# Half tiles of v copied by GpSimd, sinks' values spread in DRAM, and values' products and scores in one piece on TensorE

## The chip, the core and the metric

The kernel runs on one core of a Trainium2 chip. Its time is the device time of one launch in microseconds (us), the median of several runs. One further execution was recorded by the hardware profiler; every row below is from that one. Engines are called PE (TensorE), DVE (VectorE), ACT (ScalarE), POOL (GpSimd) and SP (SyncE, which here only issues DMAs).

## The reference

Sliding-window attention with sinks, then a feed-forward layer with a special activation:

```python
# q, k, v: (4 batches, 8 heads, 768 positions, 64); n_sink = 4, window = 128
keep   = is_sink | in_window                      # key among the first 4, or 0 <= row - key < 128
a      = softmax(where(keep, q @ k.T / 8, -1e9))
x      = (a @ v) as (3072 tokens, 512)
h      = x @ w_in                                 # 512 -> 2048
g      = h * erf(softplus(h))
out    = g @ w_out                                # 2048 -> 512
```

All is float32. Products are kept exact enough by splitting an operand into a high and a low part and adding three products.

## The kernel before

**Tiling.** Tokens go in 12 groups of 256 (three to a batch). A group's attention is 4 steps, one for each pair of heads, 48 steps in all (s = 0 to 47). A group's feed-forward layer takes 16 slices f of the hidden dimension; two slices make one tile `h` of 128x512, so a step of attention stands beside two such tiles on PE.

**A step of attention.** `score(s)` multiplies q by k into the tile `ps` (eight products on 64x64 parts of the PE array). DVE and ACT apply the mask, take the exponential and normalise. From s = 15 on (`TT`) DVE transposes blocks into the tile `turn` (line 445, and 446 for the sinks' probabilities), which goes to DRAM and comes back in another order: one DMA `pd<-turn` (line 448) and four DMAs `pa<-pd` (line 474). POOL then makes from `pa` the tile `pz` and clears the parts of `pa` that lie outside the window (lines 490 and 499; the last two instructions of a step, the "selects", write `pa`). `av(s)` multiplies these probabilities by values on 128x64 parts of the array: 4 or 6 products of `pa` with the tile `v`, then 8 of `pz` with `vz`. `vz` is one tile for all heads in which half tiles of v stand beside the sinks' values. `core(s)` issues `av(s-2)` and then `score(s)`.

**How vz is filled.** The function `dup` (lines 298 and 300) copies two halves of each step's `v` into `vz` by two DMAs on SP's queue. At the first group of a batch, line 247 loads the first 16 rows of v for two heads into eight places of `vz` by eight DMAs of 4 KB.

**The feed-forward layer.** `hidden` fills `h` by products on the whole 128x128 array (line 739), ACT and DVE compute the activation in six passes (lines 752 to 761), DVE and POOL split it into `g` (lines 768, 769), and `project` adds it into the output tile `o` (lines 784 to 786).

**Order.** A planner gives every call a due time in units of slices (`plan`, `pos(s)`) and a priority from the table `O`. A scheduler that simulates the engines then picks, on each engine, the ready instruction with the smallest due time. On the chip each engine runs its list strictly in that order, and SP issues its DMAs strictly in its own order too: a DMA that must wait holds up all that stand behind it.

Of the kernel before, what the change touches and what calls it, by code (L numbers as in the profile page):

```python
# [9 lines left out]
F32 = mybir.dt.float32  # L10
# [9 lines left out]
P = 128  # L20
SW = 16
# [23 lines left out]

TT = 15

LATE = 31

FH = 8  # L50

PW, EA = 256, 12
O = dict(prep=-100, norm=-100, core=-300, av=-300, load=-400, dup=-100, kcopy=-50, ptrans=-200, pread=-200, phalf=-150, xfin=-100,
         hid=0, proj=900, res=500, act=-400, wl=100, wc=0, ws=300)
E = dict(ptrans=-250)
UB = 4
# [4 lines left out]
def kernel(  # L61
# [74 lines left out]
    def fast_path():  # L136
        with ExitStack() as st:
# [53 lines left out]
            nc.vector.memset(vz[P // 2 :, 0], 0.0)  # L191
            nc.vector.memset(vz[: P // 2, 1], 0.0)

            pst = pers.tile([P, RING, 2, 2, KB], F32, name="pst")

            xp, early = {}, {}
# [8 lines left out]
            def load(s, what="qk"):  # L205
                g, c = divmod(s, NPAIR)
                b, gb = divmod(g, GPB)
                d = stp.setdefault(s, {})
                if "q" in what:
                    t = raw.tile([P, 2, GT], F32, tag="kq", bufs=1, name=f"kq_{s}")  # L210
                    if s >= DT:
                        d["kq"] = t
                    else:
                        d["k"], d["q"] = (t[:, j].rearrange("p (n h d) -> p n h d", n=2, h=2) for j in range(2))
                    last = start = mark.get(("d", s - 2))
                    for j, src in enumerate((k, q)):
                        if j and start is not None:
                            last = pread(s - 2, last)
                        for h in range(2):
                            if s < DT:  # L220
                                nc.sync.dma_start(
                                    d["kq"[j]][:, :, h, :],
                                    src[b, 2 * c + h, gb * GT : (gb + 1) * GT, :].rearrange("(n p) d -> p n d", p=P),
                                )
                                continue
                            for e in range(2):
                                p0 = 64 * h + 32 * e
                                x = nc.sync.dma_start(
                                    t[p0 : p0 + 32, j, :].rearrange("p (n c) -> p n c", c=32),
                                    src[b, 2 * c + h, gb * GT : (gb + 1) * GT, 32 * e : 32 * e + 32].rearrange("(n r) c -> r n c", r=32),  # L230
                                )
                                last = mark["l", s] = follow(last, x)
                if "v" in what:
                    t = d["v"] = raw.tile([P, 3, 2, D], F32, tag="v", bufs=1 + AL, name=f"v_{s}")
                    m0 = 0 if gb == 0 else 1
                    for h in range(2):
                        x = nc.sync.dma_start(
                            t[:, 1 - m0 :, h, :],
                            v[b, 2 * c + h, gb * GT - m0 * P : (gb + 1) * GT, :].rearrange("(n p) d -> p n d", p=P),
                        )  # L240
                        follow(mark.get(("l", s)), x)
                if gb == 0 and "v" in what:
                    for z in range(2):
                        for i in range(2):
                            for h in range(2):
                                r0, e = HP * (1 - z) + 2 * SW * i + SW * h, 2 * c + h
                                nc.sync.dma_start(vz[r0 : r0 + SW, z, i, e], v[b, e, :SW, :])

            def load_v(s):
                load(s, "v")  # L250
# [43 lines left out]
            def dup(s):  # L294

                g, c = divmod(s, NPAIR)
                t, cs = stp[s]["v"], slice(2 * c, 2 * c + 2)
                nc.sync.dma_start(vz[lo, 0, :, cs], t[lo, 1:])
                x = t[hi, 1:2].broadcast_to([HP, 2, 2, D]) if g % GPB == 0 else t[hi, :2]
                nc.sync.dma_start(vz[hi, 1, :, cs], x)  # L300

            def kcopy(s):

# [42 lines left out]
            def score(s, prev):  # L346
# [22 lines left out]
                for i in range(2):  # L369
                    qt = kq[:, c, 3 + i, :]  # L370
                    kt = kq[:, c].rearrange("p n t -> p (n t)")
                    runs = ((lo, KB * i, KB + 64, X[i]), (hi, KB * i + 64, KB + 80, X[i] - 80))
                    if gb + i == 0:
                        runs = ((lo, KB, KB, X[i]), (hi, KB, KB, X[i]))
                    for hf, r0, n, x in runs:
                        for h in (1, 0):
                            r = slice(64 * h, 64 * h + 64)
                            prev = follow(
                                prev,
                                nc.tensor.matmul(ps[h][hf, x : x + n], qt[r, hf], kt[r, r0 : r0 + n], start=True, stop=True),  # L380
                            )

                i0 = int(gb == 0)
                for hf, x, y in ((lo, X[0], X[0] + KB), (hi, X[0] + 64, X[0] - 80)):
# [123 lines left out]
            def av(s):  # L508

                g, c = divmod(s, NPAIR)  # L510
                d = stp[s]
                gb = g % GPB
                if s < 2:
                    a = ps_h.tile([P, 2, GT], F32, tag="h", name=f"av_{s}")[:, 0, :]
                elif s < NE:
                    a = ps_o.tile([P, DM], F32, tag="o", name=f"av_{s}")[:, :GT]
                else:
                    a = ps_t.tile([P, GT], F32, tag="t", name=f"av_{s}")
                d["av"] = a
                vt, pz = d["v"], d["pz"]  # L520
                pa = d["pa"].rearrange("p h i t -> p h (i t)")
                ops = []
                for j, (t0, t1) in enumerate(((0, HP), (HP, 3 * HP), (3 * HP, GT))):
                    if j > 0 or gb > 0:
                        x = vt[j] if isinstance(vt, list) else vt[:, j]
                        ops.append((x, pa[:, :, t0:t1], t0))
                for i in range(2):
                    for z, hf in enumerate((lo, hi)):
                        ops.append((vz[:, z, i, 2 * c : 2 * c + 2], pz[:, :, i, hf], P * i + HP * z))
                prev = mark.get(("p", s + 1)) if 0 < s < NE - 1 else None  # L530
                for m, (x, y, t0) in enumerate(ops):
                    for h in range(2):
                        o = a[64 * h : 64 * h + 64, t0 : t0 + y.shape[-1]]
                        prev = follow(
                            prev,
                            nc.tensor.matmul(
                                o, x[:, h, :], y[:, h, :], start=(m == 0), stop=(m == len(ops) - 1), skip_group_check=True
                            ),
                        )
                return prev  # L540

            def xfin(s):
# [24 lines left out]
            for s in range(NSTEP + AL):  # L567
                if s < NSTEP:
                    for what, fn, a in (
                        ("prep", prep, max(4, s - 1) if NE <= s < 2 * NPAIR else pos(s) - 3 + (s > TT)), ("norm", norm, pos(s) + 1 + (s == 1)), ("ptrans", ptrans, pos(s) + 2),  # L570
                        ("load", load, pos(s) - 4),
                    ):
                        if what == "load":
                            if s < 2 * NPAIR:
                                continue
                            plan.setdefault(a, []).append(("load", load_v, s))
                            a -= 1
                        plan.setdefault(max(a, 0 if what == "prep" else -1), []).append((what, fn, s))
                    if s >= TT:
                        if s + 2 >= NSTEP:  # L580
                            plan.setdefault(pos(s) + 3, []).append(("pread", lambda s: pread(s, mark["d", s]), s))
                        plan.setdefault(pos(s) + 5, []).append(("phalf", phalf, s))
                    if s >= 2 * NPAIR:
                        plan.setdefault(pos(s) - 2, []).append(("dup", dup, s))
                    if s // NPAIR % GPB < GPB - 1:
                        plan.setdefault(pos(s) + (2 if s < NE else 1), []).append(("kcopy", kcopy, s))
                plan.setdefault(pos(s), []).append(("core", core, s))
# [88 lines left out]
                    fn(*args)  # L676
            for z in range(2):
                plan.setdefault(0, []).append(("kcopy", lambda s: early_dup(s), z))
            plan.setdefault(2 * NE, []).append(("dup", lambda s: next_dup(), NE))
            plan.setdefault(2, []).append(("prep", lambda s: set_rest(), NSTEP))  # L680
            for m in range(-LEAD, NG * NF + LAG + 2):
# [257 lines left out]
```

## Time and profile before

| | |
|---|---|
| time, median of 3 runs | 742.46 us (742.04 to 745.74) |
| the profiled execution's own time | 743.12 us |
| its span, first to last instruction | 741.4 us |
| mean granted clock of PE | 0.986 |
| busy: PE, DVE, ACT, POOL | 95%, 74%, 67%, 34% |

How to read the rows: a row of a timeline has the start in us, the time that a merged run of equal instructions covers, engine, line, operation, tiles written and read (`out<-in`), shape and count; in brackets the idle time of the engine before it and what ended it. SPq is SP issuing a DMA. PE records one float32 product of `av` or `ps` as two instructions, so 14 products of values are 28 rows' worth. PE's instructions are pipelined: a full-array product of `o` starts 0.23 us after the one before, one of `h` 0.12 us, although each is shown as longer. PEclk 1.00 is TensorE's full clock of 2.4 GHz, 0.50 is 1.2 GHz.

### The profile page before, as it was taken

The numbers are of one execution on the slowest core, as the hardware profiler recorded it, in microseconds if no ns is written. First come the engines' busy times: TensorE is split into PE (matmuls) and PEld (weight loads), VectorE is DVE, ScalarE is ACT, GpSimd is POOL, SyncE is SP. The second block draws the span as 40 slices with busy tenths as digits, with TensorE's granted clock in tenths as the row PEclk, the third lists the DMA queues.
The fourth block names the chain that finished last, engine by engine and source line by source line (L and its number), as shares of the span: only waits on it lengthen the run. The fifth ranks groups of instructions, "written<-read, shape, count | busy, mean of one in ns | idle before, by whom it ended". The sixth has DMA issues, their size and how long they took to land. (4 is left out here: it accounts for less than half of the span.)

```text
span 741.4 us, 16223 instructions
## 1 busy us (share of the span) xinstructions
PE 703.4 (95%) x5515; PEld 573.5 (77%) x5515; DVE 545.9 (74%) x1473; ACT 494.4 (67%) x1157; POOL 253.5 (34%) x421
## 2 busy tenths in 40 slices
PE   6789998999999899899899999999999999999996
PEld 3566656787888788788688788878888878888885
DVE  6999995787777778677678768678778678664352
ACT  4686848978875576466476667577577577576572
POOL 3421302033334334343434434334524423432221
PEclk9999999999999999999999999999999999999999
DMA  7999011112244645545453553544554553420000
GB/s 177 278 352 359 18 30 54 24 31 44 65 77 102 133 103 104 113 88 92 84 130 64 104 129 70 100 110 83 102 113 85 101 125 72 85 65 1 28 1 34
DMA packets 256379, 72.87 MB, mean 98 GB/s; under 512 B 217568, under 2 KB 248928, under 8 KB 256288
## 3 DMA queue, kind: packets, MB, share of 16 engines
q1 hardware_dynamic: 255728, 71.68, 42.1%
q8 instruction: 46, 0.75, 0.4%
q14 instruction: 45, 0.37, 0.2%
q10 hardware_dynamic: 560, 0.07, 0.1%
HBM read 48.83 MB, written 17.10 MB: 89 GB/s over the span
## 5 line engine op out<-in xcount | busy, mean ns | idle before, releaser
L739 PE MATMUL h<-xh,wt 128*128 128x256 f32 x1408 | 278.6, 286 | 3.1 <-DVE u L761 2.8
L739 PEld LDWEIGHTS h<-xh,wt 128*128 128x128 f32 x1408 | 224.9, 189 | 20.8 <-issue 11.1
L739 PE MATMUL h<-xl,wt 128*128 128x256 f32 x704 | 197.8, 281 | 0.0
L757 ACT ACTIVATE u<-r 128x512 f32<-128x512 f32 x288 | 164.1, 623 | 43.0 <-DMA out_dram<-ot 25.3
L769 POOL TENSOR_TENSOR g<-u,g 128x512 fp32r<-128x512 f32 x84 | 113.2, 1347 | 217.9 <-DVE g L768 211.3
L761 DVE SCALAR_TENSOR_TENSOR u<-u,u 128x512 f32<-128x512 f32 x168 | 132.3, 788 | 26.1 <-ACT u L757 15.9
L739 PEld LDWEIGHTS h<-xl,wt 128*128 128x128 f32 x704 | 132.9, 189 | 4.6 <-issue 1.4
L784 PE MATMUL o<-wt,g 128*128 128x512 f32 x336 | 135.5, 403 | 0.7 <-DVE g L768 0.7
L785 PE MATMUL o<-wt,g 128*128 128x512 f32 x336 | 133.9, 399 | 0.0
L786 PE MATMUL o<-wt,g 128*128 128x512 f32 x336 | 132.7, 402 | 0.4 <-POOLq L907 0.2
L402 ACT ACTIVATE pst<-pst,neg 128x144 f32<-128x144 f32 x192 | 77.5, 406 | 63.9 <-DVE neg L398 63.7
L761 DVE SCALAR_TENSOR_TENSOR u<-u,h 128x512 f32<-128x512 f32 x84 | 56.7, 676 | 52.9 <-ACT u L757 52.3
L752 ACT ACTIVATE r<-h 128x512 f32<-128x512 f32 x96 | 57.0, 594 | 47.3 <-PE h L739 41.0
L786 PEld LDWEIGHTS o<-wt,g 128*128 128x128 f32 x336 | 62.8, 190 | 16.3 <-issue 1.0
L499 POOL TENSOR_SCALAR_AFFINE_SELECT pz<-pa 64x256 f32<-64x256 f32 (+1 forms) x96 | 45.4, 473 | 86.7 <-ACT pa L460 85.7
L784 PEld LDWEIGHTS o<-wt,g 128*128 128x128 f32 x336 | 63.9, 190 | 14.1 <-ACT pst L402 0.9
L785 PEld LDWEIGHTS o<-wt,g 128*128 128x128 f32 x336 | 63.8, 190 | 11.6 <-issue 0.3
L754 ACT ACTIVATE r<-r 128x512 f32<-128x512 f32 x96 | 60.4, 629 | 2.4
L753 ACT ACTIVATE r<-r 128x512 f32<-128x512 f32 x96 | 60.5, 630 | 2.2
L490 POOL COPY pz<-pa 64x256 f32<-64x256 f32 x66 | 29.2, 442 | 75.2 <-DMA pa<-pd 74.4
L417 DVE TENSOR_SCALAR pst<-pst,sum 128x128 f32<-128x128 f32 x168 | 49.9, 355 | 1.5
L380 PE MATMUL ps<-kq 64*64 64x208 f32 (+2 forms) x768 | 48.6, 360 | 1.2 <-DVE neg L398 0.7
(97 smaller groups left out, 872.6 us busy)
## 6 DMA issues: line engine op xcount, KB each, us to landing
pd<-turn SPq DMA_DIRECT2D x33, 320.0 KB, 2.7
pa<-pd SPq DMA_DIRECT2D x132, 80.0 KB, 2.6
ws<-in_moe_w_in_dram SPq DMA_DIRECT2D x16, 512.0 KB, 7.2
ws<-in_moe_w_out_dram SPq DMA_DIRECT2D x16, 512.0 KB, 8.7
out_dram<-ot SPq DMA_DIRECT2D x24, 256.0 KB, 2.4
v<-in_v_dram SPq DMA_DIRECT2D x56, 96.0 KB, 2.3
vz<-v SPq DMA_DIRECT2D x80, 64.0 KB, 2.1
kq<-in_k_dram SPq DMA_DIRECT2D x144, 32.0 KB, 2.2
```

Of the source, the lines that this page charges most:

```text
L402: mark["e", s] = nc.scalar.activation(y, y, AF.Exp, bias=d["neg"][:, i, h : h + 1], scale=-1.0, accum_out=d["sum"][:, i, h : h + 1])
L417: nc.vector.tensor_scalar_mul(p, p, sm[:, i, h : h + 1])
L739: last = nc.tensor.matmul(o, wt[NC * j + c][:, p, fs], xt[e][:, c, :], start=(m == 0), stop=(m == len(ops) - 1))
L752: nc.scalar.activation(r, h, AF.Tanh, bias=b_t, scale=0.5)
L753: nc.scalar.activation(r, r, AF.Square, bias=b_v, scale=-0.5)
L754: nc.scalar.activation(r, r, AF.Square, bias=b_r)
L757: sq = nc.scalar.activation(u, r, AF.Square, bias=b_a[i], scale=CS)
L761: pr = nc.vector.scalar_tensor_tensor(out=acc, in0=u, scalar=CC[i] * CS**2, in1=x, op0=ALU.add, op1=ALU.mult)
L769: nc.gpsimd.tensor_tensor(gl, acc, gh.bitcast(F32), op=ALU.subtract)
L784: behind(nc.tensor.matmul(o, gh[:, ws], wt[16 + f][:, 0, :], start=(f == 0), stop=False))
L785: nc.tensor.matmul(o, gh[:, ws], wt[16 + f][:, 1, :], start=False, stop=False)
L786: nc.tensor.matmul(o, gl[:, ws], wt[16 + f][:, 0, :], start=False, stop=(f == NF - 1))
```

## The change

Three edits, and a table entry with them. `set_sinks` writes `sinks` from 32 partitions of zeros (1 MB), and then the first 16 rows of v:

```diff
+NSINK = 22
...
-O = dict(prep=-100, norm=-100, core=-300, av=-300, load=-400, dup=-100, kcopy=-50, ptrans=-200, pread=-200, phalf=-150, xfin=-100,
+O = dict(prep=-100, norm=-100, core=-300, av=-300, load=-400, dup=-100, kcopy=-50, ptrans=-200, rest=-4000, pread=-200, phalf=-150, xfin=-100,
...
+            sinks = dram.tile([B * NPAIR, P // 2, 2, 2, D], F32, tag="sinks", bufs=1, name="sinks")
...
                 if gb == 0 and "v" in what:
-                    for z in range(2):
-                        for i in range(2):
-                            for h in range(2):
-                                r0, e = HP * (1 - z) + 2 * SW * i + SW * h, 2 * c + h
-                                nc.sync.dma_start(vz[r0 : r0 + SW, z, i, e], v[b, e, :SW, :])
+                    for z, hf in enumerate((hi, lo)):
+                        nc.sync.dma_start(
+                            vz[hf, z, :, 2 * c : 2 * c + 2].rearrange("p i h d -> p i (h d)"),
+                            sinks[b * NPAIR + c].rearrange("p i h d -> p i (h d)"),
+                        )
+
+            def set_sinks():
+
+                x = vz[HP : HP + 2 * SW, 0, 1].rearrange("p h d -> p (h d)").rearrange("p (o f) -> p o f", o=1)
+                nc.sync.dma_start(
+                    sinks.rearrange("n p i h d -> (n p i h d)").rearrange("(p o f) -> p o f", p=2 * SW, f=H * D),
+                    x.broadcast_to([2 * SW, B * NPAIR, H * D]),
+                )
+                for i in range(2):
+                    for h in range(2):
+                        r0 = 2 * SW * i + SW * h
+                        nc.sync.dma_start(
+                            sinks[:, r0 : r0 + SW, i, h],
+                            v.rearrange("b (c h) s d -> h (b c) s d", h=2)[h, :, :SW, :],
+                        )
...
-                nc.sync.dma_start(vz[lo, 0, :, cs], t[lo, 1:])
+                nc.gpsimd.tensor_copy(vz[lo, 0, :, cs], t[lo, 1:])
                 x = t[hi, 1:2].broadcast_to([HP, 2, 2, D]) if g % GPB == 0 else t[hi, :2]
-                nc.sync.dma_start(vz[hi, 1, :, cs], x)
+                nc.gpsimd.tensor_copy(vz[hi, 1, :, cs], x)
...
+                            with at(pos(s), "rest") if s >= TT + AL else nullcontext():
+                                prev = follow(
+                                    prev,
+                                    nc.tensor.matmul(ps[h][hf, x : x + n], qt[r, hf], kt[r, r0 : r0 + n], start=True, stop=True),
+                                )
...
+                late = s >= TT and gb > 0
...
+                if late:
+                    ops = [ops[1], ops[0], ops[2]]
...
+                        with at(pos(s), "rest") if s >= TT and m + h > 0 else nullcontext():
...
-                        plan.setdefault(pos(s) - 2, []).append(("dup", dup, s))
+                        plan.setdefault(pos(s) + 2, []).append(("dup", dup, s))
...
+            plan.setdefault(NSINK, []).append(("load", lambda s: set_sinks(), NE))
```

The two half copies become POOL instructions with a due time four slices later. The sinks' values are laid out once in DRAM, with zeros around them, and two DMAs of 64 KB a step load them in place of eight. From s = 15 on, all but the first product of `av` (and from s = 17 all products of `score`) get the priority `rest`, so that they follow the first one without other work between, and in groups with an earlier neighbour `av` begins with the product that reads the middle of `pa`, which both selects write.

The place on SP where step 26's transposes go out (`pd` is that transfer, `v_4441` or `v_4403` the values loaded ahead). Before:

```order
L474 DMA pa_4320<-pd_4323 32x20x32 x4
L228 DMA kq_4359<-in_q_dram 32x8x32 x4
L237 DMA v_4441<-in_v_dram 128x2x64 x2
L247 DMA vz<-in_v_dram 16x64 x4
L298 DMA vz<-v_4441 64x2x128
L300 DMA vz<-v_4441 64x2x128
L448 DMA pd_4535<-turn 128x5x128
```

And now:

```order
L494 DMA pa_4282<-pd_4285 32x20x32 x4
L232 DMA kq_4321<-in_q_dram 32x8x32 x4
L241 DMA v_4403<-in_v_dram 128x2x64 x2
L468 DMA pd_4491<-turn 128x5x128
L232 DMA kq_4517<-in_k_dram 32x8x32 x4
```

The transfer `pd<-turn` moved up past the two half copies, which had to wait for v to land, and past the sinks' loads.

The place on POOL where the same step's selects stand (`pz`, `pa` of step 26). Before:

```order
L490 COPY pz_4673<-pa_4532 64x4x64
L499 AFFINE_SELECT pz_4673<-pa_4532 64x2x64
L490 COPY pz_4673<-pa_4532 64x4x64
L499 AFFINE_SELECT pz_4673<-pa_4532 64x2x64
L499 AFFINE_SELECT pa_4532<-pa_4532 64x2x64 x2
L305 COPY kq<-kq 128x128
L769 TENSOR_TENSOR g_4516<-u_83_4507,g_4516 128x512
```

And now:

```order
L510 COPY pz_4629<-pa_4488 64x4x64
L519 AFFINE_SELECT pz_4629<-pa_4488 64x2x64
L519 AFFINE_SELECT pa_4488<-pa_4488 64x2x64 x2
L317 COPY vz<-v_4599 64x2x128
L319 COPY vz<-v_4599 64x2x128
L324 COPY kq<-kq 128x128
L794 TENSOR_TENSOR g_4472<-u_83_4463,g_4472 128x512
```

Two copies came in behind the selects, ahead of the next tile of `g`.

The place on PE where the values' products of step 32 stand (`av`), with the scores of step 34 (`ps`). Before:

```order
L786 MATMUL o_1_5282<-wt_1635,g_5516 128x512
L536 MATMUL av_5896<-pa_5640,v_5385 64x64 x2
L536 MATMUL av_5896<-pa_5640,v_5385 64x128 x2
L536 MATMUL av_5896<-pa_5640,v_5385 64x64
L739 MATMUL h_5809<-xh_5213,wt_1132 128x256
...
L739 MATMUL h_5809<-xh_5213,wt_1222 128x256
L536 MATMUL av_5896<-pa_5640,v_5385 64x64
L536 MATMUL av_5896<-pz_5780,vz 64x64 x8
L380 MATMUL ps_5913<-kq 64x208 x2
```

And now:

```order
L811 MATMUL o_1_5238<-wt_2239,g_5398 128x512
L560 MATMUL av_5852<-pa_5596,v_5341 64x128 x2
L560 MATMUL av_5852<-pa_5596,v_5341 64x64 x4
L560 MATMUL av_5852<-pz_5736,vz 64x64 x8
L400 MATMUL ps_5869<-kq 64x208 x2
L400 MATMUL ps_5869<-kq 64x224 x2
L400 MATMUL ps_5869<-kq 64x208 x2
L400 MATMUL ps_5869<-kq 64x224 x2
L764 MATMUL h_5657<-xh_4426,wt_1630 128x256
```

Twelve products of `h` that stood inside `av` now stand behind the scores. In the steps whose `av` stands in the stretch from 230 us on (s = 16 to 47), `av` or `score` was cut at 25 places before and is cut at one now; the scores stood apart from `av` in 12 steps and do so in 7.

## Rows read from the trace of the kernel before

**Rows 1.** The page's first part: span, and each engine's busy time

```profile
span 741.4 us, 16223 instructions
PE 703.4 (95%) x5515; PEld 573.5 (77%) x5515; DVE 545.9 (74%) x1473; ACT 494.4 (67%) x1157; POOL 253.5 (34%) x421
```

**Rows 2.** Windows: length, busy PE PEld DVE ACT POOL, PEclk, DMA share, GB/s

```profile
25.00:50.00 25.00, 22.12 (x177) 17.05 (x178) 23.64 (x60) 18.78 (x50) 9.44 (x17) 0.94 0.99 319
230.00:430.00 200.00, 189.47 (x1582) 158.95 (x1584) 148.65 (x416) 124.30 (x299) 76.51 (x137) 0.97 0.51 103
430.00:672.00 242.00, 240.35 (x1982) 203.65 (x1973) 181.00 (x481) 163.29 (x370) 96.75 (x158) 1.00 0.45 92
```

**Rows 3.** Waits: PE's of 230 to 430 us, SP's of 230 to 672

```profile
PE av L536 <- POOL pa L499: 10.0, 6, 2.9
...
SPq L298 <- DMA v<-in_v_dram: 40.7, 31, 3.0
```

**Rows 4.** Timeline of PE: two of the six late starts of av

```profile
366.18 0.91 PE L536 MATMUL av<-pa,v 128*64 128x128 f32 x8 [2.92 <-POOL pa L499]
...
424.94 0.34 PE L536 MATMUL av<-pa,v 128*64 128x64 f32 x4 [1.38 <-POOL pa L499]
```

**Rows 5.** Timeline of SP ahead of 366 us

```profile
352.33 0.91 SPq L237 DMA_DIRECT2D v<-in_v_dram  x2
353.29 3.33 SPq L247 DMA_DIRECT2D vz<-in_v_dram  x4
356.73 0.60 SPq L298 DMA_DIRECT2D vz<-v  x1
...
358.02 0.60 SPq L448 DMA_DIRECT2D pd<-turn  x1
```

**Rows 6.** Timelines of DVE and POOL, the same step

```profile
354.24 0.27 DVE L446 STREAM_TRANSPOSE turn<-turn 128x128 f32<-128x128 f32 x1
...
365.82 0.68 POOL L499 TENSOR_SCALAR_AFFINE_SELECT pa<-pa 64x128 f32<-64x128 f32 x2
```

**Rows 7.** Windows in which PE's clock is halved; columns as in rows 2

```profile
120.40:123.80 3.40, 3.40 (x17) 3.40 (x18) 2.74 (x4) 3.36 (x9) 1.46 (x3) 0.50 0.22 82
250.10:253.50 3.40, 3.40 (x16) 2.60 (x13) 1.28 (x4) 2.47 (x5) 0.50 (x1) 0.50 0.60 175
311.60:315.00 3.40, 3.31 (x31) 2.75 (x30) 1.74 (x5) 1.59 (x4) 1.90 (x4) 0.51 0.69 213
366.20:369.60 3.40, 3.40 (x28) 2.92 (x29) 2.31 (x4) 0.37 (x1) 0.29 (x1) 0.50 0.29 65
```

**Rows 8.** Timeline of PE around one step in one piece (237 us), one cut (459)

```profile
236.96 0.40 PE L786 MATMUL o<-wt,g 128*128 128x512 f32 x1
...
239.27 0.38 PE L739 MATMUL h<-xh,wt 128*128 128x256 f32 x1
...
459.07 0.40 PE L786 MATMUL o<-wt,g 128*128 128x512 f32 x1
459.40 0.66 PE L536 MATMUL av<-pa,v 128*64 128x64 f32 x10
459.99 0.39 PE L739 MATMUL h<-xh,wt 128*128 128x256 f32 x1
...
461.28 0.28 PE L739 MATMUL h<-xl,wt 128*128 128x256 f32 x1
461.39 0.28 PE L739 MATMUL h<-xh,wt 128*128 128x256 f32 x1
...
463.25 0.39 PE L739 MATMUL h<-xh,wt 128*128 128x256 f32 x1
```

**Rows 9.** POOL's copies at line 490: count, shortest, median and longest ns

```profile
L490 POOL COPY pz<-pa x66: 389/394/1030, 222.1 to 658.3; 64x256 f32<-64x256 f32 x66
```

**Rows 10.** Groups by line: DVE's first pass over a weight block

```profile
L635 DVE TENSOR_SCALAR wf<-ws 128x512 int32<-128x512 int32 x32 | 14.6, 460 | 0.4 <-DMA ws<-in_moe_w_out_dram 0.4
```

**Rows 11.** Waits of PE over the whole span: one in the start

```profile
PE tp L454 <- DVE pst L417: 2.3, 1, 2.3
```

More of the change, by code (lines that the diff above doesn't have):

```diff
@@ L377, in score @@
                             r = slice(64 * h, 64 * h + 64)
[L378 to L381, printed above, removed]
+                            with at(pos(s), "rest") if s >= TT + AL else nullcontext():
[3 more added lines that the diff above has]
+                                )
                 i0 = int(gb == 0)
@@ L533, in av @@
                         o = a[64 * h : 64 * h + 64, t0 : t0 + y.shape[-1]]
[L534 to L539, printed above, removed]
+                        with at(pos(s), "rest") if s >= TT and m + h > 0 else nullcontext():
+                            prev = follow(
+                                prev,
+                                nc.tensor.matmul(
+                                    o, x[:, h, :], y[:, h, :], start=(m == 0), stop=(m == len(ops) - 1), skip_group_check=True
+                                ),
+                            )
                 return prev
```

## The prediction

> **What bounds the kernel now.** I read the page's first part, then windows, then the waits of PE and of SP, then the timelines around PE's longest waits.
>
> PE is busy for 703 of 741 us and DVE for 74% [rows 1], so PE's list of instructions sets the end, and a gain must come from PE's gaps or from its instructions standing closer. The windows show two late stages [rows 2]: from 230 to 430 us PE idles for 200 - 189.5 = 10.5 us at a clock of 0.97, from 430 to 672 for only 1.7 us at 1.00. DVE is at 148.65 / 200 = 74% and 181 / 242 = 75% there, ACT below it: neither is at its limit when PE runs without gaps.
>
> The 10.5 us have one cause: 10.0 of them are six waits of `av` for POOL's writing of `pa`, the longest 2.9 us [rows 3]; the two at 425 us belong to one step, so five steps are late. The latest starts at 366.18 [rows 4]. I follow it back. POOL's two selects begin at 365.82 [rows 6], right behind the landing of `pa`. DVE had finished this step's transposes at 354.24 + 0.27 = 354.51 [rows 6], but SP issued `pd<-turn` only at 358.02 [rows 5]: 3.5 us late, more than the stall of 2.92. Ahead of it SP loaded v at 352.33, spent from 353.29 to 356.73 on four sinks' loads and on waiting for v to land, and issued two half copies of 0.60 each [rows 5]. Over the 31 steps between 230 and 672 us SP waited 40.7 us in that place for v, 1.3 a step [rows 3]. So the queue of SP, not DVE or POOL, was last in this chain.
>
> After three of the late starts PE's clock stood at half for 3.4 us [rows 7], as it did once in the start.
>
> **The change part by part.** The sum is made against the profiled execution, 743.1 us (741.4 of span [rows 1] and 1.7 around it).
>
> *The half copies leave SP.* Each step takes two issues of 0.60 and a mean wait of 1.3 off SP, 2.5 us, all ahead of `pd<-turn`; in the group's first steps of a batch six of eight sinks' issues as well. In step 26 the orders show nothing left between v's load and `pd`, so `pd` goes out when DVE is done and the selects end up to 3.5 us earlier: that stall goes. The other four are of the same kind: three shorter ones at whose steps the diff takes away the same two copies and the wait, and the last one, at 424.94, where 1.38 and a further 0.4 are to be covered by 2.5. Against that stand POOL's new copies, two a step ahead of later work and in some steps between the two selects. The row nearest to them is line 490's copy of the same 64x256 elements: 0.39 us at the shortest and in the median, 1.03 at the longest [rows 9]. I take 0.39, 0.8 a step, which adds 80 x 0.39 = 31 us to POOL's 253.5 (38% of the span), with idle time around it. Of the 10.0 us I count 8 as gone and 2 as kept: bounds 0, if something else is last in every step, and 10.
>
> *The clock.* A stretch of 3.4 us at half clock loses 1.7 us; three are 5.1 us [rows 7]. The start at 424.94, late by 1.38, was followed by no fall: no half-clock stretch of the trace lies behind it, and from 430 us on the clock is 1.00 [rows 2, 4]. Stalls shortened to that size or less should leave the clock alone: 5.1 us gone, bounds 0 and 5.1.
>
> *One piece on PE.* A step in one piece takes from the start of the last product before it (236.96) to the first one after it (239.27) 2.31 us. The same work with one cut takes 459.99 - 459.07 = 0.92 and 463.25 - 461.39 = 1.86, together 2.78 [rows 8]. The cut has one more full-array product inside, whose spacing is 461.39 - 461.28 = 0.11 (0.12 over the run). So a cut costs 2.78 - 2.31 - 0.12 = 0.35 us: going from the whole array to parts of it and back is paid once more. The orders lose 24 cuts (25 before, one now): 24 x 0.35 = 8.4 us. Scores that stand apart from `av` fall from 12 to 7; between `av` and `ps` the parts change anyway, so I count 0.1 each, an estimate between 0 and the 0.35 of a cut: 0.5 us. These 8.9 us lie on PE's own list, so nothing hides them; bounds 7 (cuts at a pair of products may cost less) and 10.
>
> *What is late next.* One piece must wait for both selects, since it begins with the product that reads what both write. Before, work of `h` stood between. From 430 us on `av` can have waited for very little, since PE's whole idle time there is 1.7 us [rows 2], although SP stopped for v in those steps too; with 2.5 us less on SP it should not begin to. A further 1.7 + 0.5 us of idle is left to other waits.
>
> *The start.* The zeros written for `sinks` are 1 MB, placed ahead of a weight block while the DMA engines are 99% busy at 319 GB/s [rows 2]: 1.05 MB / 319 GB/s = 3.3 us. DVE's passes over the blocks waited 0.4 us in all for them [rows 10], so the transfers are just ahead there, and DVE is 95% busy; the delay can cost 0 to 3.3 us. Half of PE's slack in that window (2.9 of 25) takes some of it: I take +1. The scheduler also moved products of the start about, in one step to alternating `ps` and `av`; I take 0, with bounds of -4 (below) and +3.
>
> Sum: 743.1 - 8 - 5.1 - 8.9 + 1 = 722.1. The profiled execution lies 0.7 above the median of the timed runs, so 721.4; I say 722.
>
> **Rivals.**
>
> *The stalls stay (A).* The chain behind `pa` has two transfers and POOL, and another link could be last as soon as SP is not. Then only the pieces count: 743.1 - 8.9 + 1 - 0.7 = 734.5. For it: the steps with little slack were ordered by a scheduler that puts `av` where it believes `pa` to be ready, so it may pull the next step just as tight. Against: in step 26 the 3.5 us are plainly SP's.
>
> *POOL's copies hold up DVE (B).* The row of line 490 has a longest copy of 1.03 against a median of 0.39 [rows 9], so POOL and DVE do get in each other's way. If each new copy held DVE for its 0.39 us, the transposes of the 14 tight steps (s = 17 to 30) would come 0.8 later and PE's `av` with them: 14 x 0.8 = 11 us. That gives 722.1 + 11 - 0.7 = 732. Against it: DVE has a quarter of its time free. The Trainium skill (SBUF — State Buffer, section Who interferes with whom) says that GpSimd and VectorE share one pair of SBUF ports as an exclusive lock, and that the later one is blocked for the whole instruction. By that rule the copies would not be free for DVE, though a DMA in their place was; the trace agrees as far as the 1.03 goes, and no row shows how long DVE was held.
>
> *The start gains as well (C).* PE's wait of 2.3 us for a transpose's operand [rows 11] is followed by the half clock at 120.4 [rows 7]; the order puts these transposes later now. If both go, and the zeros hide: 722.1 - 2.3 - 1.7 - 1 - 0.7 = 716.
>
> *One piece waits (D), slower than before.* With a cut, 461.39 + 0.12 - 459.99 = 1.5 us of other products ran while the second select was still due [rows 8]. If in the 30 steps from s = 18 the selects ended only at that point, PE would stand for 30 x 1.5 = 45 us: 743.1 - 8.9 + 45 + 1 - 0.7 = 780. It decides from 22 / 30 = 0.7 us a step. POOL's copies between the selects (0.8) speak for it, the gapless 430 to 672 us against it.
>
> **How the numbers follow.** Forecast 0.60 (own range 717 to 729), A 0.16, B 0.06, C 0.11, D 0.07. Within 0.5%, 3.7 us, is what a measurement of this kernel can't tell from no change. Faster is all of the forecast and of C, and most of A and B: 0.88. Same takes the rest of A and B, where the start costs its full 3.3 too: 0.06. Slower is D with little of it elsewhere: 0.06. The range of 713 to 736 holds the forecast, A, B and C, and leaves out D.
>
> **What would show it.** Right: no wait of `av` for `pa` over 1.5 us after 230 us; the clock at 1.00 from 230 us to the end of the attention; SP issuing `pd<-turn` within 0.1 us of DVE's last transpose in most steps; one piece of about 2.3 us a step; POOL at 38% or 39%. Wrong: half-clock windows still behind late starts of `av` (A); DVE's passes at line 761 longer than before and transposes later (B); idle time in front of `av` in most steps after 430 us (D); a wait on a weight block at 40 us over 3 us (the start).

## The result, and the profile after

The changed kernel takes 722.83 us, the median of four runs (719.08 to 724.46), against 743.3 of the kernel before beside it. The ratio is 0.9714, its 95% interval 0.9667 to 0.976: faster by 2.9%. The forecast was 722, range 713 to 736. The profiled execution is the shortest of the four, 719.08 us, so the traces differ by 24.0 us where the medians differ by 20.5.

The page's first part, which answers to [rows 1]:

```profile
span 717.4 us, 16180 instructions
PE 690.8 (96%) x5515; PEld 568.0 (79%) x5515; DVE 550.5 (77%) x1473; ACT 493.2 (69%) x1157; POOL 291.6 (41%) x501
```

POOL has the 80 copies more (421 to 501 instructions) and 38.1 us more work, DVE the same 1473 instructions and 4.6 us more.

Windows, the columns as in [rows 2]: the crowded start, two stretches that stand for those of before, and the only one with a halved clock ahead of the span's last microseconds ([rows 7] had four after 100 us):

```profile
25.00:50.00 25.00, 19.52 (x166) 14.89 (x161) 19.90 (x48) 18.09 (x46) 8.73 (x16) 0.93 0.99 292
215.00:415.00 200.00, 196.32 (x1712) 166.84 (x1711) 162.53 (x451) 131.12 (x317) 99.45 (x181) 1.00 0.52 106
415.00:650.00 235.00, 233.29 (x1979) 201.85 (x1978) 182.92 (x481) 161.82 (x369) 108.50 (x188) 1.00 0.42 86
46.70:50.10 3.40, 3.40 (x8) 2.77 (x9) 3.31 (x7) 2.20 (x4) 1.22 (x2) 0.50 1.05 401
```

PE idles for 3.7 of 200 us where it idled for 10.5, and the clock stays at 1.00. The start got worse: PE is busy for 19.52 of 25 us, before for 22.12.

PE's waits from 238.3 to 627.3 us (the stretch is explained below), the answer to [rows 3]:

```profile
PE ps L400 <- DVE kq L341: 1.9, 2, 1.2
PE o L811 <- POOL g L794: 1.2, 1, 1.2
PE h L764 <- DVE u L786: 1.1, 1, 1.1
PE o L809 <- DVE g L793: 0.6, 1, 0.6
PE av L560 <- POOL pa L519: 0.6, 1, 0.6
```

The wait of `av` for `pa` fell from 10.0 us to 0.6. Of the other four only that of `h` for `u` stood in this stretch before (1.9 us); those for `kq` and `g` are new. SP's longest wait from 215 to 660 us:

```profile
SPq L468 <- DVE turn L466: 109.7, 29, 7.3
```

SP stood for v before; now it stands ready for DVE, in 29 steps. The step that [rows 5] and [rows 6] show is the transpose that starts at 346.63 here; DVE and SP, one row each:

```profile
346.63 0.30 DVE L466 STREAM_TRANSPOSE turn<-turn 128x128 f32<-128x128 f32 x1
```

```profile
346.95 0.37 SPq L468 DMA_DIRECT2D pd<-turn  x1
```

`pd` is issued 346.95 - 346.93 = 0.02 us behind the transpose's end, where it was 3.51. Over all 33 such transposes the issue comes more than 0.1 us late in two (0.14 and 0.82).

A step in one piece on PE, the answer to [rows 8]:

```profile
386.26 0.40 PE L811 MATMUL o<-wt,g 128*128 128x512 f32 x1
386.59 0.67 PE L560 MATMUL av<-pa,v 128*64 128x128 f32 x12
387.09 0.64 PE L560 MATMUL av<-pz,vz 128*64 128x64 f32 x16
387.66 0.99 PE L400 MATMUL ps<-kq 64*64 64x208 f32 x16
388.58 0.38 PE L764 MATMUL h<-xh,wt 128*128 128x256 f32 x1
```

From start to start 388.58 - 386.26 = 2.32 us, before 2.31.

POOL's new copies by line, with mean ns, against [rows 9]:

```profile
L319 POOL COPY vz<-v 64x256 f32<-64x256 f32 x40 | 19.3, 484 | 1.8
L317 POOL COPY vz<-v 64x256 f32<-64x256 f32 x40 | 18.4, 459 | 40.7 <-DMA v<-in_v_dram 38.2 <-PE av L560 1.9
```

They take 37.7 us, not 31: the mean (0.47) lies above the median of 0.39 that the forecast used, and POOL is busy for 41% where 38 or 39 was forecast. The wait for v, 38.2 us, is now POOL's. Little is held up by it: the waits that the trace puts down to the copies are 1.5 us on POOL itself and 1.1 us of PE's weight loads.

The start's waits from 20 to 130 us:

```profile
DVE wf L659 <- DMA ws<-in_moe_w_out_dram: 4.6, 1, 4.6
...
PE h L760 <- DVE gf L786: 3.5, 1, 3.5
```

The zeros delay a weight block: DVE waits 4.6 us for it (0.4 for all blocks in [rows 10]), PE 3.5 behind DVE, and the half clock at 46.7 follows. The wait of [rows 11] and the half clock at 120.4 are gone, though.

### The profile page after: what moved, and what is told of

Same layout as the page of the kernel before. It is cut to its first block, busy times and chain, and to the rows that moved or that the text cites. A ratio compares the mean times of both kernels' runs of the same rounds, so it can differ in the third digit from the quotient of the medians.

```text
span 717.4 us, 16180 instructions
## 1 busy us (share of the span) xinstructions
PE 690.8 (96%) x5515; PEld 568.0 (79%) x5515; DVE 550.5 (77%) x1473; ACT 493.2 (69%) x1157; POOL 291.6 (41%) x501
## 3 DMA queue, kind: packets, MB, share of 16 engines
HBM read 50.27 MB, written 18.42 MB: 96 GB/s over the span
## 5 line engine op out<-in xcount | busy, mean ns | idle before, releaser
L764 PE MATMUL h<-xh,wt 128*128 128x256 f32 x1408 | 273.2, 284 | 1.1 <-DVE u L786 1.1
L764 PEld LDWEIGHTS h<-xh,wt 128*128 128x128 f32 x1408 | 222.6, 188 | 15.6 <-issue 8.4
L786 DVE SCALAR_TENSOR_TENSOR u<-u,u 128x512 f32<-128x512 f32 x168 | 134.8, 802 | 20.2 <-ACT u L782 7.1
L809 PE MATMUL o<-wt,g 128*128 128x512 f32 x336 | 134.1, 399 | 1.2 <-DVE g L793 1.2
L811 PE MATMUL o<-wt,g 128*128 128x512 f32 x336 | 131.2, 398 | 1.6 <-POOL g L794 1.4
L810 PE MATMUL o<-wt,g 128*128 128x512 f32 x336 | 132.7, 395 | 0.0
L811 PEld LDWEIGHTS o<-wt,g 128*128 128x128 f32 x336 | 62.3, 187 | 17.8 <-POOL g L794 2.3
L519 POOL TENSOR_SCALAR_AFFINE_SELECT pz<-pa 64x256 f32<-64x256 f32 (+1 forms) x96 | 47.6, 496 | 69.1 <-ACT pa L480 68.0
L809 PEld LDWEIGHTS o<-wt,g 128*128 128x128 f32 x336 | 63.0, 187 | 14.9 <-DVE g L793 1.1
L810 PEld LDWEIGHTS o<-wt,g 128*128 128x128 f32 x336 | 63.0, 188 | 11.4 <-issue 0.3
L793 DVE CAST g<-u 128x512 fp32r<-128x512 f32 x84 | 37.0, 440 | 22.2 <-PE o L811 18.0
L400 PE MATMUL ps<-kq 64*64 64x208 f32 (+2 forms) x768 | 51.5, 362 | 2.4 <-DVE kq L341 1.9
```

Of the source, the lines that this page charges most:

```text
L764: last = nc.tensor.matmul(o, wt[NC * j + c][:, p, fs], xt[e][:, c, :], start=(m == 0), stop=(m == len(ops) - 1))
L786: pr = nc.vector.scalar_tensor_tensor(out=acc, in0=u, scalar=CC[i] * CS**2, in1=x, op0=ALU.add, op1=ALU.mult)
L809: behind(nc.tensor.matmul(o, gh[:, ws], wt[16 + f][:, 0, :], start=(f == 0), stop=False))
L810: nc.tensor.matmul(o, gh[:, ws], wt[16 + f][:, 1, :], start=False, stop=False)
L811: nc.tensor.matmul(o, gl[:, ws], wt[16 + f][:, 0, :], start=False, stop=(f == NF - 1))
```

## The experiments

To set kernels side by side I use one stretch that does about the same work in each: from ACT's copy of the third group's output to that of the tenth (seven groups of four steps). In before and after:

```profile
238.50:650.10 411.60, 399.42 (x3304) 335.64 (x3302) 309.51 (x853) 263.83 (x622) 162.49 (x279) 0.99 0.49 100
```

```profile
238.30:627.30 389.00, 383.62 (x3324) 329.07 (x3320) 314.46 (x855) 262.63 (x622) 188.33 (x337) 1.00 0.47 97
```

22.6 of the 24.0 us lie in it. PE's idle time falls from 411.6 - 399.4 = 12.2 us to 5.4, its busy time by 15.8. The other kernels' rows follow; "idle" is length less PE's busy time, "half clock" the length of the stretches with a granted clock of 0.50, and "late pd" counts, out of 33 transposes, those behind which SP issues `pd` more than 0.5 us late, and in brackets the lateness of all 33 in sum:

```
kernel       ratio to before [interval]   length  PE busy  idle  half clock  late pd (sum us)
before       1                            411.6   399.4    12.2  10.2        17 (52.8)
pieces_only  0.9983 [0.9952, 1.0014]      409.5   390.3    19.2  10.2        19 (45.6)
no_pool      0.987  [0.9831, 0.9909]      401.3   387.9    13.5   6.8        12 (21.1)
sp_load      0.9777 [0.9742, 0.9811]      396.6   385.7    10.9   3.4         8 (16.4)
queue_again  0.9772 [0.974, 0.9804]       394.5   393.8     0.7   0           1 (2.2)
no_sinks     0.9735 [0.9703, 0.9768]      391.9   383.9     8.0   0           4 (5.8)
after        0.9714 [0.9667, 0.976]       389.0   383.6     5.4   0           1 (1.9)
after_again  0.9721 [0.9689, 0.9753]      388.8   383.6     5.2   0           1 (1.8)
```

**The queue without the pieces** (twice, the second time beside the changed kernel again on one chip):

```
-  with at(pos(s), "rest") if s >= TT + AL else nullcontext():   # scores
+  with nullcontext():
-  late = s >= TT and gb > 0
+  late = False
-  with at(pos(s), "rest") if s >= TT and m + h > 0 else nullcontext():   # av
+  with nullcontext():
```

> The changed kernel with POOL's copies of v and the sinks' two loads, but without the one-piece rule on PE (no priority rest, av begins with its old first product). Theory (two separate gains: a shorter SP queue takes PE's waits for pa and the half clock, about 14 us; pieces take the cuts, about 8.5): waits of av for pa under 3 us after 230 us, no half clock after 130 us, some 25 cuts still there, time 729 to 733. Rival (the pieces alone did it, because scores come earlier and so the whole chain to pa): waits for pa stay near 10 us, time 740 to 745.

> The changed kernel without the rule that puts values' products and scores in one piece (POOL's copies and the two sinks' DMAs stay). Forecast's sum: after + 8.9 us, about 731. Theory after the first runs: after + 3 to 5 us, about 726, with PE's waits of av for pa under 1 us in all and no half clock after 60 us.

> The changed kernel once more, on the same chip and against the same runs of before as the next three: the base of their differences. By its first runs the ratio to before is 0.967 to 0.976, some 722 us. Both theories expect that; what is read from it is its distance to the kernel without the one piece (queue_again). The forecast's sum: 8.9 us less than that one. The theory after the first four runs (a cut costs little by itself, and most of the gain is that PE no longer stands for pa): 3 to 5 us less.

Measured: 726.5 us (ratio 0.9763 [0.9735, 0.9791]), the second time 726.44, and 722.05 for the changed kernel beside it. The window of the second one:

```profile
240.60:635.10 394.50, 393.78 (x3315) 332.44 (x3312) 308.20 (x853) 263.56 (x621) 186.88 (x338) 1.00 0.46 95
```

PE's only wait in it:

```profile
PE o L811 <- POOL g L794: 0.5, 1, 0.5
```

Of the 12.2 us of idle 11.5 go, where the forecast counted 8, and the half clock goes whole. So the queue, the clock and what the start loses come to 742.32 - 726.44 = 15.9 us. The pieces take a further 393.78 - 383.56 = 10.2 us of PE's work away, as forecast (8.9), but bring 5.2 - 0.7 = 4.5 us of idle back, and the time moves by 726.44 - 722.05 = 4.4 (the stretch by 394.5 - 388.8 = 5.7).

**The pieces without the queue** (before, with the changed rule for `av` and scores; the copies stay on SP, the sinks with eight DMAs):

```
+  rest=-4000 ...
+  late = s >= TT and gb > 0
+  if late: ops = [ops[1], ops[0], ops[2]]
+  with at(pos(s), "rest") if ... (av and scores)
```

> The kernel before with the one-piece rule alone: v's halves still copied by two DMAs on SP, sinks' values by eight. Theory of two separate gains: SP still issues pd<-turn 1 to 4 us after DVE's last transpose, PE waits 8 to 14 us for pa with two or three half-clock stretches, time 733 to 737. Rival (pieces alone): waits for pa under 3 us, time 721 to 726. A third way (one piece waits for the last select with SP late): waits of over 15 us, time 742 or more.

Measured: 743.07 us, no change. The window, and PE's waits from 235 to 655 us:

```profile
240.60:650.10 409.50, 390.33 (x3296) 332.31 (x3288) 309.19 (x848) 262.52 (x621) 159.52 (x279) 0.99 0.49 100
```

```profile
PE av L560 <- DMA v<-in_v_dram: 6.4, 2, 4.7
PE av L560 <- POOL pa L519: 4.6, 6, 2.4
PE o L808 <- DVE g L792: 3.6, 3, 1.5
PE h L763 <- DVE u L785: 1.7, 3, 1.0
PE ps L400 <- DVE kq L341: 1.7, 3, 0.7
PE o L810 <- POOL g L793: 1.4, 2, 0.7
```

PE's work falls by 9.1 us, and its idle time grows by 7.0. The first row names v, but both starts lie 0.05 us or less behind the end of POOL's last select, as those of the second row do (251.12 and 313.06, the selects' ends at 250.17 + 0.90 = 251.07 and 312.12 + 0.90 = 313.02), so they too are waits for `pa`. In all `av` then waits 11.0 us, where before it waited 10.0 from 235 to 655 us. Most of the growth is new waits for `g`, 5.0 us, and for `kq`, 1.7: with less work in its list PE comes to operands that DVE and POOL have not made yet. The other 2.1 us are lost in the start, where the third group ends at 240.6 and not at 238.5. Taking work off the engine that is busy for 95% bought nothing as long as what it waits for came late.

**What makes SP late.** Three kernels, all with the pieces. The first issues the half copies from SP again, at their old place; the second loads the sinks with eight DMAs again and writes no zeros; the third is the changed kernel with two spare DMAs a step on SP that read v where the copies did, so SP waits for v, but nobody waits for them.

```
no_pool:   - nc.gpsimd.tensor_copy(vz[lo, 0, :, cs], t[lo, 1:])   (and the other half)
           + nc.sync.dma_start(vz[lo, 0, :, cs], t[lo, 1:])
           - plan.setdefault(pos(s) + 2, []).append(("dup", dup, s))
           + plan.setdefault(pos(s) - 2, []).append(("dup", dup, s))
no_sinks:  + the loop of eight v loads into vz;  - set_sinks()
sp_load:   + nc.sync.dma_start(w[0], t[lo, 1:]); nc.sync.dma_start(w[1], t[hi, ...])   at pos(s) - 2
```

> The changed kernel with the half copies issued by SP again, at their old place in the order; the pieces and the two sinks' DMAs a step stay. Theory 1: the two copies and the wait for v in front of them make SP late, so SP waits for v again by some 40 us in 30 steps, PE waits for pa by 6 us or more, the clock falls behind such a wait, and the time is 735 to 743. Theory 2: the six sinks' issues a step are what makes SP late, so the time stays at 722 to 728 and PE's waits for pa under 2 us.

> The changed kernel with eight sinks' DMAs in each first step of a batch again, straight from v; no zeros and no sinks in DRAM; POOL's copies and the pieces stay. Theory 1 (copies and the wait carry the gain): 721 to 727. Theory 2 (the sinks' issues carry it): 733 to 743, with pd<-turn issued some 2 us or more behind DVE's last transpose in the steps with sinks and PE's waits for pa there.

> The changed kernel, and two more DMAs a step on SP at the old place of the half copies, from the tile v to an unused DRAM tile: SP again waits for v to land and issues two DMAs ahead of pd<-turn; vz is still filled by POOL. Theory (SP's lateness is what made av wait): the wait of SP for v returns to 30 us or more, PE's wait for pa to 5 us or more with at least one half clock, time 729 to 736. Rival (the new, even spacing of av by itself has enough slack): waits for pa under 2 us, time 721 to 725.

Measured: 733.95, 723.24 (both beside 742.32 of before) and 726.74 (beside 744.79). Of the first, SP's wait for v and PE's for `pa`, from 235 to 655 us, and its two stretches at half clock:

```profile
SPq L317 <- DMA v<-in_v_dram: 50.6, 33, 3.3
```

```profile
PE av L560 <- POOL pa L519: 6.9, 6, 3.0
```

```profile
311.80:315.20 3.40, 3.40 (x35) 3.28 (x36) 0.16 (x1) 0.79 (x2) 0.00 (x0) 0.50 0.53 182
431.20:434.60 3.40, 3.40 (x17) 3.31 (x16) 3.24 (x8) 3.25 (x10) 1.28 (x1) 0.50 0.04 10
```

Of the third, the same two waits:

```profile
SPq L326 <- DMA v<-in_v_dram: 49.1, 32, 3.5
```

```profile
PE av L568 <- POOL pa L527: 3.1, 4, 1.4
```

The copies carry most of the gain: with them back on SP the changed kernel loses 733.95 - 722.05 = 11.9 us, waits for `pa` return, and the clock falls twice. The first fall stands behind a wait for `pa` that ends at 311.78 (3.00 us); the second does not: ahead of it PE waited twice for `g` (1.52 us to 428.70, 0.73 to 430.15). no_pool takes back both the engine and the place in the order; whether two DMAs on SP at the new, later place would have done as well as POOL's copies, no run here shows.

The sinks' DMAs are worth 1.2 us beside POOL's copies, which can't be told from nothing, but 0.9983 - 0.987 = 1.1% or some 8 us where the copies stay on SP (no_pool against pieces_only). The 1.2 has two sides: no_sinks is 391.9 - 388.8 = 3.1 us longer in the stretch, and its start, which has neither the zeros nor the step in turns shown below, is shorter (the third group ends at 236.4, in the changed kernel at 238.3 and 240.9). The two parts relieve the same queue, and either one covers much of what the other would.

In the table the five kernels with pieces line up: the less late `pd` is, the less time they take. The spare DMAs cost 0.6% (0.9777 against 0.9721), in the stretch 396.6 - 388.8 = 7.8 us, with a wait for v as long as no_pool's. The time is below what the theory of a late SP had expected, and so is the wait for `pa` (3.1 us, not 5). The test is not a pure one, since the spare DMAs also write 23.66 - 18.42 = 5.2 MB more to DRAM. The rest of no_pool's loss can be that SP is later there (21.1 us in sum against 16.4), the order around the copies or their landing in `vz`, and these runs don't separate the three.

**The start.** Three kernels: the scores' rule from step 8 on (in the changed kernel one step of the start has scores and products in turn), the zeros behind the last weight load, and both.

```
fix_rest:    - with at(pos(s), "rest") if s >= TT + AL ...
             + with at(pos(s), "rest") if s >= 2 * NPAIR ...
zeros_late:  + mark["w"] = nc.sync.dma_start(t, ...)          (each weight load)
             + follow(mark["w"], nc.sync.dma_start(sinks, zeros))
```

> The changed kernel with the scores' priority of the one piece given from step 8 on, not from step 16 on: on PE only the one step of the start changes in which scores and values' products alternate product by product (6.73 us at 97 to 99 us of the span in every kernel with zeros and sinks; 2.29 where they don't alternate). Theory 1 (PE's list sets the end there too): 4.4 us less than after, 717 to 719. Theory 2 (the forecast's 0: what follows waits for other engines, so the time goes into a wait behind): 720 to 723, and a wait of PE that is new or longer before 220 us.

> The changed kernel with the zeros for the sinks in DRAM written behind the last load of a weight block. Theory 1 (the zeros delay a weight block and with it DVE and PE by 3 to 5 us): DVE's wait for the block and PE's wait for gf at 43 us go, and the start to the third group's end comes out 2 to 4 us earlier, 718 to 720 in all. Theory 2 (the start has other limits, as the kernel with both changes of the start showed): both waits go, and the time is 720 to 727 since other waits of the start take their place.

> The changed kernel with two edits in the start: the zeros for sinks are written behind the last weight load, and scores get the priority rest from s = 8 on, so that no step alternates single products of scores and values. Theory (the start paid for both: DVE waited 4.6 us for a weight block where it waited 0.4 before, and the alternating step took 6.7 us of PE where 2.3 were needed): DVE's wait back to under 1 us, no step over 2.5 us of PE in the start except for waits, time 713 to 719. Rival (the start is set by DVE's passes over the weights, so PE's part of it is free): time 721 to 724.

Measured: 719.29 us (ratio 0.9664 [0.9629, 0.9698]), 718.76 (0.9675 [0.9638, 0.9712]) and, for both together, 726.94 (0.9754 [0.9706, 0.9801]). Of the changed kernel, the first and the last rows of the step in which scores and products take turns; of fix_rest the same step:

```profile
93.46 3.17 PE L806 MATMUL o<-wf,gf 128*128 128x512 f32 x7
96.56 0.56 PE L400 MATMUL ps<-kq 64*64 64x208 f32 x2
97.05 0.33 PE L560 MATMUL av<-pa,v_early 128*64 128x64 f32 x2
...
102.62 0.68 PE L560 MATMUL av<-pz,vz 128*64 128x64 f32 x14
103.23 0.66 PE L347 MATMUL tqk<-ident,kq 128*128 128x128 f32 x4
```

```profile
98.17 0.99 PE L400 MATMUL ps<-kq 64*64 64x208 f32 x16
99.09 0.67 PE L560 MATMUL av<-pa,v_early 128*64 128x64 f32 x12
99.59 0.64 PE L560 MATMUL av<-pz,vz 128*64 128x64 f32 x16
100.16 0.66 PE L347 MATMUL tqk<-ident,kq 128*128 128x128 f32 x4
```

The 22 products, 44 rows' worth, take 103.23 - 96.56 = 6.67 us in turn and 100.16 - 98.17 = 1.99 apart. The ratio falls by 0.57%, some 4 us, but how much of the step's gain reached the end isn't settled: the third group ends at 237.4, where the changed kernel's two profiles have 238.3 and 240.9. The forecast had put this at 0. With the zeros late, the waits for the block fall from 4.6 and 3.5 us to 0.7 each, the third group ends at 236.4 (238.3 in after, 240.9 in its second profile), and a wait of before is back:

```profile
PE tp L474 <- DVE pst L437: 2.3, 1, 2.3
```

```profile
119.10:122.50 3.40, 3.37 (x15) 2.98 (x15) 3.19 (x7) 3.39 (x8) 0.50 (x1) 0.50 0.29 96
```

Both together miss: the third group ends at 243.5, with 6.8 us of half clock at 120, and nothing of either gain is left. Each edit lets the program's scheduler set the start anew, and here the gains of the start did not add up. The two single kernels have the lowest ratios of all. They did not run beside the changed kernel, and their intervals touch its own (0.9689 at the lower end), so half a per cent is likely and not settled.

## Why the prediction was right, and where it was not

- **The half copies leave SP.** Right in the mechanism and too small in size: 8 us were counted; without the pieces 11.5 of 12.2 us of idle went. The 1.9 us in which `h` waited for `u` went with those for `pa`. The prediction took copies and sinks together; the runs show that they cover for each other, so that the sinks' DMAs are worth 8 us or 1. One reading was loose: POOL's selects at 365.82 don't stand right behind the landing of `pa`. POOL's first copy from `pa` starts at 364.15, and 1.7 us of its work come before the selects.
- **The clock.** Right: 10.2 us at half clock in the stretch before, none after, 5.1 us. That only waits for `pa` bring the clock down was not shown: no_pool gives two stretches back and sp_load one, and of these three one stands behind a wait for `pa`, the others behind waits of `o` for `g` (2.09 us in sp_load).
- **One piece on PE.** Right in size on PE (8.9 forecast, 9.1 and 10.2 measured in busy time), wrong as a gain in time: "nothing hides them" did not hold, since nearly half of it, and without the queue's relief all of it, went into other waits and the start.
- **What is late next.** This is the step that failed. It left 2 + 2.2 us of idle whether the pieces came or not, since nothing waited after 430 us. The queue alone leaves 0.7, and the pieces bring 4.5 back, in waits for `kq`, `u` and `g` of DVE and POOL. The forecast's split was 12.1 for queue, clock and start and 8.9 for the pieces; measured are 15.9 and 4.4. By the other order of the two edits the split is another: the pieces alone buy nothing (0.9983), and the queue added to them buys the whole (0.9721). The two misses of 3.8 and 4.5 us cancel, so the sum was right to a microsecond by luck as much as by working.
- **The start.** +1 was close on balance (the third group ends at 238.3 and 240.9, before at 238.5), with parts far from it: the zeros held PE for 3.5 us, beyond the bound of 3.3 that was to hold if nothing hid them, and the sign named for this, a wait on the weight block over 3 us, came. The turns cost PE 4.7 us, beyond their bound of 3, and by the ratios the time some 4. Against both stand the 2.3 and 1.7 us of [rows 11] and [rows 7], which rival C had named.
- **Rivals.** A is out: the stalls went. no_pool comes out near its time, but there SP stays late in 12 steps, and a part of the stalls with it. D is out: in after `av` waits 0.6 us for `pa`, and in pieces_only 11.0, where it was 10.0; the idle time that the pieces bring stands in front of other instructions. B is out as told: queue_again has the same copies on POOL, DVE's busy time is 308.2, before 309.5, and PE waits 0.5 us in all.

DVE's time does grow where both come in, to 314.5 and 317.7 us in the two profiles of the changed kernel. The copies alone don't do it, nor do the pieces alone (309.2 in pieces_only, 309.8 in no_pool). A part of the growth shows at one line. The passes that read two tiles of SBUF lengthen a little, from 788 ns on average to 802, and to 828 in after_again; those that read `h` from PSUM don't (676 and 672). In before, and then in after:

```profile
L761 DVE SCALAR_TENSOR_TENSOR u<-u,u 128x512 f32<-128x512 f32 x168 | 132.3, 788 | 26.1 <-ACT u L757 15.9 <-ACT r L754 0.5
```

```profile
L786 DVE SCALAR_TENSOR_TENSOR u<-u,u 128x512 f32<-128x512 f32 x168 | 134.8, 802 | 20.2 <-ACT u L782 7.1 <-DVE u L786 0.5
L786 DVE SCALAR_TENSOR_TENSOR u<-u,h 128x512 f32<-128x512 f32 x84 | 56.5, 672 | 44.8 <-ACT u L782 44.7
```

Two such passes on DVE, and what POOL ran beside them:

```profile
314.25 2.36 DVE L786 SCALAR_TENSOR_TENSOR u<-u,u 128x512 f32<-128x512 f32 x2
```

```profile
314.48 1.58 POOL L794 TENSOR_TENSOR g<-u,g 128x512 fp32r<-128x512 f32 x1 [1.10 <-DVE g L793]
```

In the trace of after a pass over two tiles takes 0.69 us with nothing on POOL (84 of the 168), 1.14 on average beside POOL's pass over `g` (40), and 0.74 with only a copy of v beside it (4). The passes that read `h` take 0.67 us alone (34 of 84) and 0.68 beside `g` (35). So the neighbour that costs DVE time is the old pass, and the new copies meet few passes. Why the old pass costs more where both edits come in, these runs don't show. The Trainium skill (SBUF — State Buffer, Who interferes with whom) states that a DVE instruction with two SBUF inputs contends with a GpSimd instruction that reads SBUF, and one with a single SBUF input outside the two-port modes doesn't; the means 1.14 and 0.68 us beside the same pass of POOL agree.

## What to carry to other kernels

Before counting what an edit takes off the busiest engine, ask what stood in for it: work that is cut out between two waits may have been hiding the second one, and then the wait takes its place. Compare the moment an operand is ready with the moment its DMA is issued, step by step; an issue queue that is late in half of the steps is worth clearing first, and two edits that clear the same queue don't add up. Where a scheduler sets the order, run each part alone, since a small edit can move the far end of the program by more than it is worth itself.

## What was not expected of the hardware

Scores and products of values in turn, one by one, cost PE 6.67 us where the same 22 products apart took 1.99: 4.68 us more for the changes between two forms that both use part of the array. Each of the first eight turns of one score and one product of values takes some 0.75 to 0.88 us (96.56 to 97.31, 98.06 to 98.94).

The forecast took starts that are late by 1.4 us or less as harmless to the clock. One row speaks against it: in fix_rest PE waits twice within 2.3 us, and the granted clock stands at half from 527.9 to 531.3. PE's timeline, and that window:

```profile
525.55 0.50 PE L809 MATMUL o<-wt,g 128*128 128x512 f32 x1 [0.69 <-DVE g L793]
...
527.84 0.52 PE L764 MATMUL h<-xh,wt 128*128 128x256 f32 x1 [1.10 <-DVE u L786]
```

```profile
527.90:531.30 3.40, 3.40 (x16) 3.40 (x17) 3.26 (x6) 3.31 (x11) 2.58 (x4) 0.50 0.00 0
```

Neither wait is as long as the 1.38 us of [rows 4], behind which no fall came. The lengths of such waits don't tell, though: in no_pool PE waits 1.52 us to 540.39 and 1.10 to 542.68 for the same two operands, and in after 0.60 to 525.95 and 1.10 to 528.25, and the clock stays at 1.00 behind both pairs. What decides between them, these runs leave open.
